# Moving the operands of an expert layer's matmuls within SBUF: four pools, each with a pad of its own

## The chip, the cores and the metric

The kernel runs on one core of a Trainium2 chip. The metric is device time in microseconds of one execution. Three executions of the kernel before gave 1094.63, 1095.49 and 1096.83 us; the median, 1095.49 us, is what the change is compared with. TensorE is called PE below, with PEld for its loads of stationary operands; VectorE is DVE, ScalarE ACT, GpSimd POOL and SyncE SP.

## The reference

Causal attention with two sparse masks (half of the heads see the last 32 positions, the other half every 32nd), and behind it a mixture of 8 experts in which each token goes to its best two:

```python
scores = np.where(masks[None], scale * np.matmul(q, k.transpose(0, 1, 3, 2)), -1e9)
attn = softmax(scores)                       # q, k, v: (8, 8, 576, 64)
x = np.matmul(attn, v)  ->  (4608, 512)      # one row per token
top2, top2_w = best two of  x @ w_gate + log1p(exp(x @ w_noise)) * noise
for e in range(8):
    for k in range(2):
        mask = top2[:, k] == e
        h = np.maximum(x[mask] @ w1[e], 0.0)              # 512 -> 1024
        out[mask] += top2_w[mask, k, None] * (h @ w2[e])  # 1024 -> 512
```

All inputs and the output are float32.

## The kernel before

**Two parts on one instruction stream.** The attention of 8 batches, with the routing of each batch behind it, and the experts are cut into pieces (class `Piece`), and `issue_all` (L291 to L406) puts them out in an order worked out from planned durations and dependences. Where a tile lies in memory is no input to that order. Attention ends near 330 us; from there on the experts' matmuls alone fill PE. Some jobs of the first three experts run earlier, between the attention's pieces.

**A job** is a part of one expert's list of tokens, 256 to 384 rows wide. The rows are gathered by indirect DMA on POOL's queue into `xg` (L971), turned by DVE into `xr` (L1010), and split into two float32r halves: `xhi` is the value rounded by ACT's cast (L1017), `xlo` the rest, by DVE (L1019). Weights come from HBM on SP's queue into `wraw` and are split in the same way into `w1hi`, `w1lo`, `w2hi`, `w2lo` (L894, L895).

**Layer 1** (L1048): for each of the 8 slices f of 128 hidden columns, 12 matmuls into one PSUM bank: for each d of 4, (w1hi, xhi), (w1hi, xlo), (w1lo, xhi). The 128x128 piece of the weights is the stationary operand, the 256 to 384 tokens are the moving one. Where the job has a tail, the program reads the list's length and runs the ten inner matmuls of the 12 at one of three widths. ACT then writes `hhi` (relu, L1067), DVE `hlo` (L1072).

**Layer 2** (L1110): for each block of 128 tokens, 24 matmuls into one bank: for each f of 8, (hhi, w2hi), (hhi, w2lo), (hlo, w2hi). Here 128 columns of h are stationary and 512 columns of w2 move. DVE weighs the result (L1135), POOL's queue scatters it (L1140).

So the x tiles and the w2 tiles are moving operands, the w1 tiles and the h tiles are stationary.

**Where the tiles lie.** SBUF pools stand one behind the other in the order in which they are opened, tiles within a pool in the order of their first use, and each tile takes a multiple of 32 bytes per partition. In the program before, the pools that matter are `wring` (`wraw`, `w1hi`, `w1lo`, `w2hi`, `w2lo`; all tiles 2048 bytes per partition) and behind it `ffn` (the lists, `xg`, `xhi`, `xlo`, `hhi`, `hlo`, `prev`, `xr`). The places of the matmul operands, as bytes behind a multiple of 128:

| operand | role | first byte before | behind a multiple of 128 |
|---|---|---|---|
| w1hi, w1lo | stationary, layer 1 | 111,264 | 32 |
| xhi, xlo | moving, layer 1 | 181,184 | 64 |
| hhi, hlo | stationary, layer 2 | 193,472 | 64 |
| w2hi, w2lo | moving, layer 2 | 144,032 | 32 |

All these tiles are a multiple of 128 bytes long, and so is every step by which a matmul's slice starts within one (a slice of 128 columns is 512 bytes, a slice d of x 1536), so each row of the table holds for every matmul.

Of the kernel before, what the change touches and what calls it, by code (L numbers as in the profile page):

```python
# [9 lines left out]
F32 = mybir.dt.float32  # L10
F32R = mybir.dt.float32r
# [11 lines left out]
def kernel(  # L23
# [31 lines left out]
    NF = FF // 128  # L55
# [92 lines left out]
    actx = ctx.enter_context(ExitStack())  # L148
    keep = actx.enter_context(tc.tile_pool(name="keep", bufs=1))
    wring = actx.enter_context(tc.tile_pool(name="wring", bufs=4))  # L150
    ffn = actx.enter_context(tc.tile_pool(name="ffn", bufs=1))
    psum = actx.enter_context(tc.tile_pool(name="psum", bufs=1, space=PSUM))

    kT_l = keep.tile([128, STRIDE + S], F32, name="kT_l")
# [70 lines left out]
    def ring(pool, shape, dtype, name, k):  # L225
        return Ring(k, make=lambda: pool.tile(shape, dtype, name=name, bufs=k))
# [189 lines left out]
    R = {}  # L416
# [452 lines left out]
    for name, shape, dtype, depth in (  # L869
            ("tabt", [128, 3, 3], I32, 3), ("gix", [128, 3], I32, 3), ("tabx", [128, 12, 3], I32, 2),  # L870
            ("gxx", [128, 3, 4], I32, 2), ("xg", [128, 4, 128], F32, 2), ("xr", [128, ND * 128], F32, 1),
            ("xhi", [128, ND, WID], F32R, 1), ("xlo", [128, ND, WID], F32R, 1),
            ("hhi", [128, WID], F32R, NF), ("hlo", [128, WID], F32R, NF),
            ("prev", [128, DM], F32, 4)):
        R[name] = ring(ffn, shape, dtype, name, depth)
    for layer in (1, 2):
        for part in ("hi", "lo"):
            R[f"w{layer}{part}"] = ring(wring, [128, 512], F32R, f"w{layer}{part}", NF)
    R["wraw"] = ring(wring, [128, 512], F32, "wraw", 5)
    ER = 1000000  # L880
    ZC = 384
# [407 lines left out]
```

## Time and profile before

| | before |
|---|---|
| time, median of 3 (lowest to highest) | 1095.49 us (1094.63 to 1096.83) |
| span of the profiled execution | 1098.7 us |
| PE busy | 1062.6 us, 97% of the span |
| matmuls on PE | 8637, of which the experts' (L1048 and L1110) are 3072 and 1792 |
| DVE, POOL, ACT busy | 607.4, 566.9 and 435.3 us |

The profiled execution is one of its own, 3.2 us above the median. A busy PE is not PE at its peak: a matmul counts from its start until its result has left the array, so one begins while the one before still counts as busy. How fast PE goes is read from the distance between starts. The chain of work that ended last lists which instruction, or which wait, set the end, in order of time. A line of a timeline gives start and duration in us, then engine, line, operation, tiles written and read, and sizes (K by M of the stationary operand, then the result).

### The profile page before, as it was taken

The numbers are of one execution on the slowest core, as the hardware profiler recorded it, in microseconds if no ns is written. First come the engines' busy times: TensorE is split into PE (matmuls) and PEld (weight loads), VectorE is DVE, ScalarE is ACT, GpSimd is POOL, SyncE is SP. The second block draws the span as 40 slices with busy tenths as digits, with TensorE's granted clock in tenths as the row PEclk, the third lists the DMA queues.
The fourth block names the chain that finished last, engine by engine and source line by source line (L and its number), as shares of the span: only waits on it lengthen the run. The fifth ranks groups of instructions, "written<-read, shape, count | busy, mean of one in ns | idle before, by whom it ended". The sixth has DMA issues, their size and how long they took to land.

```text
span 1098.7 us, 23347 instructions
## 1 busy us (share of the span) xinstructions
PE 1062.6 (97%) x8637; PEld 938.2 (85%) x8637; DVE 607.4 (55%) x1604; ACT 435.3 (40%) x1135; POOL 566.9 (52%) x741
## 2 busy tenths in 40 slices
PE   8898998999999999999999999999999999999995
PEld 7677787788889888989998989898988898898994
DVE  6688988686573236536673455345534653373341
ACT  5689988775552114214341233123312331141120
POOL 1044543552535556647676556554656464657520
PEclk8998899999999999999999999999999999999998
DMA  7899999998653324424553236224522452253210
GB/s 167 216 214 222 245 220 222 207 240 236 171 166 104 100 75 142 153 72 146 176 177 108 75 107 184 73 71 121 171 79 66 126 164 75 76 153 97 78 50 23
DMA packets 169710, 152.95 MB, mean 139 GB/s; under 512 B 52879, under 2 KB 137359, under 8 KB 169576
## 3 DMA queue, kind: packets, MB, share of 16 engines
q1 hardware_dynamic: 145160, 92.31, 33.5%
q0 software_dynamic: 24416, 58.87, 17.5%
q8 instruction: 82, 1.34, 0.5%
q14 instruction: 52, 0.43, 0.1%
HBM read 112.78 MB, written 39.39 MB: 138 GB/s over the span
## 4 chain that ended last, share of the span: by engine, by line
PE 87%; ACT 5%; DMA 4%; DVE 2%; issue 1%; POOL 0%; SPq 0%; POOLq 0%; DVEq 0%; ACTq 0%
PE bankB L1110 6%; PE bankG L1110 6%; PE bankE L1110 5%; PE bankE L1048 5%; PE bankC L1048 5%; PE bankF L1048 5%; PE bankD L1048 5%; PE bankA L1048 5%; PE bankB L1048 5%; PE bankC L1110 5%; PE bankH L1048 5%; PE bankD L1110 5%; PE bankG L1048 5%; PE bankF L1110 4%; PE bankH L1110 4%; PE bankA L1110 4%
## 5 line engine op out<-in xcount | busy, mean ns | idle before, releaser
L971 POOL DMA_INDIRECT xg<-x_dram,gxx x248 | 254.7, 1027 | 110.0 <-issue 56.5
L1140 POOL DMA_INDIRECT out_dram<-prev,tabt x80 | 82.4, 1030 | 100.9 <-DVE prev L1135 46.8
L824 POOL DMA_INDIRECT tab<-ent,addr x96 | 94.0, 979 | 64.0 <-issue 18.5
L1088 POOL DMA_INDIRECT prev<-out_dram,gix x80 | 78.6, 982 | 91.5 <-issue 36.2
L1010 DVE STREAM_TRANSPOSE xr<-xg 128x512 f32<-128x512 f32 (+1 forms) x66 | 68.6, 1040 | 11.3 <-DMA xg<-x_dram,gxx 10.0
L1017 ACT CAST xhi<-xr 128x512 fp32r<-128x512 f32 (+1 forms) x66 | 39.0, 592 | 72.3 <-DVE xr L1010 72.3
L894 ACT CAST w2hi<-wraw 128x512 fp32r<-128x512 f32 x80 | 47.1, 619 | 25.4 <-PE bankA L1119 7.4
L895 DVE TENSOR_TENSOR w1lo<-wraw,w1hi 128x512 fp32r<-128x512 f32 x80 | 54.8, 687 | 2.8 <-ACT w1hi L894 0.2
L895 DVE TENSOR_TENSOR w2lo<-wraw,w2hi 128x512 fp32r<-128x512 f32 x80 | 52.7, 684 | 5.1 <-ACT w2hi L894 4.7
L1019 DVE TENSOR_TENSOR xlo<-xr,xhi 128x512 fp32r<-128x512 f32 (+1 forms) x66 | 43.5, 659 | 19.2 <-ACT xhi L1017 17.9
L894 ACT CAST w1hi<-wraw 128x512 fp32r<-128x512 f32 x80 | 49.0, 615 | 0.1
L812 POOL COPY ent<-wt 96x12 f32<-96x12 f32 x8 | 1.6, 196 | 89.2 <-DVE wt L806 89.2
L1048 PE MATMUL bankE<-xhi,w1hi 128*128 128x256 f32 (+3 forms) x132 | 39.8, 301 | 0.0
L1067 ACT ACTIVATE hhi<-bankC 128x256 fp32r<-128x256 f32 (+2 forms) x32 | 13.7, 428 | 65.0 <-PE bankC L1048 65.0
L1048 PE MATMUL bankE<-xhi,w1lo 128*128 128x256 f32 (+3 forms) x132 | 39.4, 299 | 0.0
L1048 PE MATMUL bankE<-xlo,w1hi 128*128 128x256 f32 (+3 forms) x132 | 39.3, 298 | 0.0
L1067 ACT ACTIVATE hhi<-bankA 128x256 fp32r<-128x256 f32 (+2 forms) x32 | 13.6, 424 | 63.6 <-PE bankA L1048 62.6
L1048 PE MATMUL bankC<-xhi,w1hi 128*128 128x256 f32 (+3 forms) x128 | 38.6, 302 | 0.0
L1048 PE MATMUL bankH<-xhi,w1hi 128*128 128x256 f32 (+3 forms) x128 | 38.6, 301 | 0.0
L1067 ACT ACTIVATE hhi<-bankH 128x256 fp32r<-128x256 f32 (+2 forms) x32 | 13.5, 423 | 62.7 <-PE bankH L1048 62.7
L1048 PE MATMUL bankF<-xhi,w1hi 128*128 128x256 f32 (+3 forms) x128 | 38.4, 300 | 0.0
L1048 PE MATMUL bankD<-xhi,w1hi 128*128 128x256 f32 (+3 forms) x128 | 38.4, 300 | 0.0
(660 smaller groups left out, 3640.5 us busy)
## 6 DMA issues: line engine op xcount, KB each, us to landing
wraw<-in_moe_w_dram SPq DMA_DIRECT2D x160, 256.0 KB
out_dram<-zeros SPq DMA_DIRECT2D x12, 768.0 KB
ks<-in_k_dram SPq DMA_DIRECT2D x15, 320.0 KB
qs<-in_q_dram SPq DMA_DIRECT2D x15, 320.0 KB
vraw<-in_v_dram SPq DMA_DIRECT2D x30, 160.0 KB
raw<-in_k_dram SPq DMA_DIRECT2D x16, 288.0 KB
v_l<-in_v_dram SPq DMA_DIRECT2D x16, 288.0 KB
raw<-in_q_dram SPq DMA_DIRECT2D x16, 288.0 KB
```

The lines of the kernel that those rows point to most:

```text
L824: st = nc.gpsimd.indirect_dma_start(out=tab, out_offset=bass.IndirectOffsetOnAxis(ap=s["addr"].t[:, t, kk:kk + 1], axis=0), in_=s["ent"].t ...
L894: Piece("ACT", act(512) + 30, lambda o: nc.scalar.copy(hi.t, raw.t), rank, read=[raw], alloc=[hi], expert=True)
L895: Piece("DVE", dve(512), lambda o: nc.vector.tensor_tensor(lo.t, raw.t, hi.t.bitcast(F32), ALU.subtract), rank, read=[raw, hi], alloc=[lo] ...
L971: dma(lambda o, g=g: nc.gpsimd.indirect_dma_start(out=xg.t[:, g, :], out_offset=None, in_=x_dram[:4 * known, :], in_offset=bass.IndirectOf ...
L1010: Piece("DVE", 8 * rows, lambda o, xg=xg, xr=xr, ng=ng, rows=rows: nc.vector.transpose(xr.t.rearrange("p (c x) -> p c x", c=ND)[:, :, :row ...
L1017: Piece("ACT", act(4 * rows), lambda o, view=view, cols=cols: nc.scalar.copy(xh.t[:, :, cols], view()), rank, read=[xr], expert=True, **{h ...
L1019: Piece("DVE", dve(4 * rows), lambda o, view=view, cols=cols: nc.vector.tensor_tensor(xl.t[:, :, cols], view(), xh.t[:, :, cols].bitcast(F ...
L1048: nc.tensor.matmul(ps.t[:, :width], a.t[:, 128 * d:128 * d + 128], c.t[:, d, :width], start=(m == 0), stop=(m == len(todo) - 1))
L1067: Piece("ACT", act(width) + 30, lambda o: nc.scalar.activation(hh.t[:, :width], ps.t[:, :width], AF.Relu), rank, read=[ps], alloc=[hh], ex ...
L1088: dma(lambda o: nc.gpsimd.indirect_dma_start(out=pv.t[:rows, :], out_offset=None, in_=out[:known, :], in_offset=bass.IndirectOffsetOnAxis( ...
L1110: nc.tensor.matmul(ps.t, HT[n, f][p[0]].t[:, cols], W2[n][f][p[1]].t, start=(m == 0), stop=(m == len(todo) - 1))
L1140: st = nc.gpsimd.indirect_dma_start(out=out[:known, :], out_offset=bass.IndirectOffsetOnAxis(ap=tb.t[:rows, i, 0:1], axis=0), in_=pv.t[:ro ...
```

## The change

The pool `wring` is split: `w2hi` and `w2lo` go to a pool of their own, `w2ring`. The pool `ffn` is split: `hhi` and `hlo` go to `hpool`. Each of the four pools gets, as its first tile, a pad of one partition that nothing writes or reads: 32 bytes in `wring`, 64 in `w2ring`, 96 in `ffn`, 128 in `hpool`. No instruction is added, taken away or moved, and no tile changes its size or number of buffers.

```diff
     wring = actx.enter_context(tc.tile_pool(name="wring", bufs=4))
+    w2ring = actx.enter_context(tc.tile_pool(name="w2ring", bufs=1))
     ffn = actx.enter_context(tc.tile_pool(name="ffn", bufs=1))
+    hpool = actx.enter_context(tc.tile_pool(name="hpool", bufs=1))
+    for pool, name, words in ((wring, "shift_w1", 8), (w2ring, "shift_w2", 16), (ffn, "shift_x", 24),
+                              (hpool, "shift_h", 32)):
+        pool.tile([1, words], F32, name=name, bufs=1)
     psum = actx.enter_context(tc.tile_pool(name="psum", bufs=1, space=PSUM))
...
-        R[name] = ring(ffn, shape, dtype, name, depth)
-    for layer in (1, 2):
+        R[name] = ring(hpool if name in ("hhi", "hlo") else ffn, shape, dtype, name, depth)
+    for layer, pool in ((1, wring), (2, w2ring)):
         for part in ("hi", "lo"):
-            R[f"w{layer}{part}"] = ring(wring, [128, 512], F32R, f"w{layer}{part}", NF)
+            R[f"w{layer}{part}"] = ring(pool, [128, 512], F32R, f"w{layer}{part}", NF)
```

## The prediction

> **What bounds the kernel now.** First the page: the busy shares and the chain of work that ended last.
>
> ```profile
> span 1098.7 us, 23347 instructions
> PE 1062.6 (97%) x8637; PEld 938.2 (85%) x8637; DVE 607.4 (55%) x1604; ACT 435.3 (40%) x1135; POOL 566.9 (52%) x741
> PE 87%; ACT 5%; DMA 4%; DVE 2%; issue 1%; POOL 0%; SPq 0%; POOLq 0%; DVEq 0%; ACTq 0%
> ```
>
> PE makes 87% of the chain, but an average hides stages. So next the table by stretches, whole, then for layer 1 (L1048) and for layer 2 (L1110) alone, cut at 330 us, where attention ends:
>
> ```profile
> core 0: us, PE busy (x) PEld busy (x) DVE busy (x) ACT busy (x) POOL busy (x), PEclk, DMA share, GB/s
> 0.00:330.00 330.00, 306.90 (x4212) 257.25 (x4213) 249.70 (x976) 237.69 (x719) 130.95 (x257) 0.95 0.87 210
> 330.00:1098.00 768.00, 755.70 (x4427) 680.99 (x4425) 357.70 (x629) 197.57 (x417) 435.90 (x484) 1.00 0.36 109
> ...
> 0.00:330.00 330.00, 45.02 (x291) 40.43 (x292) 0.95 0.87 210
> 330.00:1098.00 768.00, 379.29 (x2783) 376.70 (x2781) 1.00 0.36 109
> ...
> 0.00:330.00 330.00, 44.72 (x168) 29.90 (x168) 0.95 0.87 210
> 330.00:1098.00 768.00, 383.94 (x1624) 303.76 (x1624) 1.00 0.36 109
> ```
>
> Behind 330 us PE is busy 755.7 of 768 us at full granted clock (1.00); the 12.3 us that lack are the end, behind the last matmul. No other engine is over 57% busy there, and the experts' matmuls fill the stretch (379.3 + 383.9 us). Ahead of 330 us, DMA is at 0.87 of its engines and only 459 of these matmuls run. So the question is whether one of the experts' matmuls becomes shorter or longer. Nothing else of the change can count for much.
>
> Busy time doesn't say how fast PE goes; the distance between starts does. From the timeline, the first matmul of a bank and the first of the next (12 matmuls later), for widths 384, 320 and 256, and 12 matmuls of layer 2 with width 512:
>
> ```profile
> 329.58 0.34 PE L1048 MATMUL bankC<-xhi,w1hi 128*128 128x384 f32 x1
> 331.66 0.34 PE L1048 MATMUL bankB<-xhi,w1hi 128*128 128x384 f32 x1
> ...
> 409.80 0.31 PE L1048 MATMUL bankG<-xhi,w1hi 128*128 128x320 f32 x1
> 411.55 0.31 PE L1048 MATMUL bankE<-xhi,w1hi 128*128 128x320 f32 x1
> ...
> 699.83 0.40 PE L1110 MATMUL bankD<-w2hi,hlo 128*128 128x512 f32 x1
> 702.63 0.40 PE L1110 MATMUL bankD<-w2hi,hlo 128*128 128x512 f32 x1
> 702.87 0.28 PE L1048 MATMUL bankC<-xhi,w1hi 128*128 128x256 f32 x1
> 704.27 0.28 PE L1048 MATMUL bankB<-xhi,w1hi 128*128 128x256 f32 x1
> ```
>
> The chain shows the same as whole groups (start, length, engine, bank, line, matmuls):
>
> ```profile
> 340.14 2.08 PE bankA L1048 x12
> ...
> 411.72 1.76 PE bankE L1048 x12
> ...
> 461.20 5.60 PE bankD L1110 x24
> ```
>
> One matmul takes 2.08/12 = 173.3 ns at 384 columns, 1.76/12 = 146.7 at 320, 1.40/12 = 116.7 at 256, and 5.60/24 = 233.3 at 512. From 320 to 384 columns a column costs 26.7/64 = 0.417 ns, so 384 columns should take 160.0. **13.3 ns of each of these matmuls don't depend on the width.** By the same 0.417 ns a column, 13.3 ns are 32 columns, and 32 columns of 4 bytes are a run of 128 bytes in each partition. At 256 columns the excess is 116.7 - 106.7 = 10.0 ns (three quarters of such a run), at 512 it is 233.3 - 213.3 = 20.0 ns (one and a half). Over all matmuls of the two lines, counted by width (1856 of 256, 288 of 320, 768 of 384, 160 of 288, which is near enough to 320 to go with it; 1792 of 512), that is 18.6 + 16.2 + 35.8 = 70.6 us.
>
> **Where the excess sits.** The last matmul ahead of a gap in the loads shows whether a stationary operand that is being loaded holds up the matmul that streams beside it:
>
> ```profile
> 238.21 0.34 PE L1048 MATMUL bankC<-xhi,w1hi 128*128 128x384 f32 x1
> 238.21 0.19 PEld L1048 LDWEIGHTS bankC<-xlo,w1hi 128*128 128x128 f32 x1
> ...
> 238.56 0.34 PE L1048 MATMUL bankC<-xhi,w1lo 128*128 128x384 f32 x1
> ...
> 238.83 0.20 PEld L617 LDWEIGHTS bankA<-v_s,aT 72*64 72x64 f32 x4 [0.26 <-ACT w2hi L894]
> ```
>
> The matmul at 238.21 has a load beside it, the one at 238.56 has none for 0.27 us. Both last 0.34 us; without 13.3 ns the second would show 0.33. So the excess belongs to the moving stream, not to a meeting with the next load. The table of places says what differs between the layers: x starts 64 bytes behind a multiple of 128, w2 starts 32 behind. A moving operand of n whole runs of 128 bytes that starts off such a multiple touches n + 1 of them. That is just the one run of excess in layer 1, and it is the reading on which I forecast.
>
> **The change part by part.** No instruction comes, goes or moves; each pad has no reader and no writer. What moves is the place of tiles. `wring` began at 101,024, 32 bytes behind a multiple of 128; with its pad of 32, `wraw`, `w1hi` and `w1lo` stand at 64. Their 21 tiles of 2048 bytes end at 144,064, and 64 bytes later w2 stands at 144,128, at 0. It ends at 176,896; with 96 of pad, 192 for `tabt` and 96 for `gix`, `xg` stands at 177,280, and x at 181,376, at 0. `hpool` begins at 204,352, and h at 204,480, at 64. So the change does what its words say; that it doesn't I leave out of the chances.
>
> The price of a matmul after it: the least that can stay above the columns' time I take from a place where attention's transposes run one behind the other, 128 columns each:
>
> ```profile
> 23.40 0.60 PE L688 MATMUL bankG<-ident,xo 128*128 128x128 f32 x4
> ...
> L688 PE MATMUL bankG<-ident,xo x4: 270/272/275, 23.4 to 23.7; 128*128 128x128 f32 x4
> ```
>
> (a line of the timeline, then the same four with their least, median and greatest ns). The fourth starts 600 - 272 = 328 ns behind the first, so they follow at 109 ns; 256 steps of 0.417 are 106.7 ns (such a float32 column takes two steps), and some 2.5 ns stay. So one run of 13.3 ns goes at 288 to 384 columns down to 2.5 (10.8 saved), at 256 the whole 10.0 down to 2.5 (7.5 saved), at 512 one run of the one and a half (13.3 saved, 6.7 stay: I don't know what the half is). The bounds of each saving are what it would be at 2.5 ns left everywhere (17.5 at 512), and below nothing as in the rivals. The sum: 1856 x 7.5 = 13.9 us, 1216 x 10.8 = 13.1 us, 1792 x 13.3 = 23.9 us, together 50.9.
>
> Of this, 459 of 4864 matmuls, about 4.8 us, lie ahead of 330 us among attention's waits, where DMA's 0.87 may take back what PE saves; I count half. That leaves 48.5 us, and 1098.7 - 48.5 = 1050.2 us of span. The median of the runs lies 3.2 us below this profiled span: **1047 us**.
>
> What is late next? PE's own waits are short and all in attention, the longest sum being
>
> ```profile
> PE bankG L688 <- DVE xo L641: 3.5, 2, 3.2
> ```
>
> so nothing is near to holding PE behind 330 us: the rewriting of x and w1 for the next job lies beside three blocks of layer 2 (16.8 us, then about 15.8), and takes DVE at most 8 casts of weights,
>
> ```profile
> L895 DVE TENSOR_TENSOR w1lo<-wraw,w1hi 128x512 fp32r<-128x512 f32 x80 | 54.8, 687 | 2.8 <-ACT w1hi L894 0.2
> ```
>
> 5.5 us. The other tiles that move (`wraw`, `xg`, `xr`, `prev`) are read and written by DMA, ACT and DVE, which have 57% of load or less behind 330 us; I cost them at nothing. Ahead of it that cover is thin: were all DMA there 1% slower or faster, that would be about 3 us either way.
>
> The Trainium skill speaks against this change. "TensorE: Matmul & The Clock Gate", Part 2, says that PE has two independent read ports, so that loading the next stationary operand takes nothing from the running matmul. The two rows at 238 us agree, 0.34 us with and without a load, and by that rule the stationary side of the change is worth nothing. "SBUF — State Buffer", Specifications, gives 16 bytes as the unit in which SBUF is read; 0, 32 and 64 are all multiples of 16, so by that page nothing changes at all, which is the second rival below. The first page's section on the back-to-back gap gives N/2.4 + 2.5 ns, 215.8 at 512 columns, where the rows here have 233.3; an estimate with it for all widths would give 58 us of saving, and 1040 us.
>
> **The rivals.**
> - **No change, 1095.5 us.** The excess is a fixed cost of such a matmul. For it: 256 and 512 columns cost the same per column (0.456 ns), though x and w2 lie at different places, and the excess there is no whole number of runs. Against: exactly one run at 320 and 384.
> - **Only places off a multiple of 64 cost.** Then x at 64 was well placed before, and only w2 (at 32) gains: half a run, 1792 x 6.7 = 12.0 us, or a whole one, 23.9; less half of the early tenth, 1084 or 1073 us. For it: layer 2 has the greater excess.
> - **Slower, 1115 us.** The extra half run of layer 2 comes with its stationary operand at 64, where layer 1 has it at 32. The change puts w1 at 64 as well, so all 3072 matmuls of layer 1 would pay 6.7 ns more: 20.5 us, less half of the early tenth 19.5. This decides if the moving operand's place turns out to be worth nothing and the stationary one's is not. For it: 20.0 against 13.3 ns, which the moving place alone doesn't explain. Against: the matmul at 238.56.
>
> **How the numbers follow.** Forecast 0.40, no change 0.28, only off 64 0.13, slower 0.19. The forecast's own range is 1036 (all down to 2.5 ns, early ones too: 58.4 us saved, and 1 us for the scatter of runs) to 1060 (the 256-column matmuls keep their excess: 13.9 us less saved). The range over 8 in 10 runs from there to the top of no change, 1098; the slower case stays outside. A measurement of this kernel tells 0.2%, about 2 us, from no change. Faster 0.53, same 0.28, slower 0.19.
>
> **What would show it.** In the profile after, a group of 24 in layer 2 takes about 5.28 us instead of 5.60, one of 12 at 384 columns 1.95 instead of 2.08, at 256 about 1.31 instead of 1.40. Unchanged groups mean the first of the rivals; 5.28 to 5.44 with 2.08 kept means the second; 2.16 at 384 columns the third. The forecast is wrong in its second step if the groups shrink and the span doesn't: then a wait on PE must have appeared behind 330 us.

## The result, and the profile after

| | before | after |
|---|---|---|
| time, median of 13 runs | 1096.83 us | 1092.37 us |
| ratio after / before | | 0.9947, 95% interval 0.9924 to 0.9969 |
| span of the profiled execution | 1098.7 us | 1095.7 us |

The change makes the kernel faster by 0.5%: by the ratio, which compares runs that stand beside each other, 5.8 us of 1096.83 (3.4 to 8.3 by its interval); the two medians alone differ by 4.5. The forecast was 48.5 us, to 1047. The 13 runs before include the three given further up. The ratios here and below leave out one execution of 2057 us after, another of 2057 us of `both_best`, and one of 1433 us of the kernel before beside it, and no trace shows what held these up.

The page after, and then the same three views by stretches as before: whole, layer 1 (now L1053), layer 2 (now L1115).

```profile
span 1095.7 us, 23347 instructions
PE 1060.5 (97%) x8637; PEld 943.4 (86%) x8637; DVE 607.3 (55%) x1604; ACT 435.9 (40%) x1135; POOL 562.6 (51%) x741
...
330.00:1095.00 765.00, 752.65 (x4438) 684.41 (x4436) 358.47 (x632) 198.15 (x418) 435.12 (x488) 1.00 0.36 110
...
330.00:1095.00 765.00, 381.04 (x2784) 378.64 (x2784) 1.00 0.36 110
...
330.00:1095.00 765.00, 379.38 (x1634) 305.29 (x1632) 1.00 0.36 110
```

PE still fills everything behind 330 us (752.7 of 765 us, the rest being the end), and nothing new waits there. So nothing was gained and then lost: the matmuls themselves hardly became shorter. The chain shows by how much (start, length, engine, bank, line, matmuls):

```profile
425.97 5.51 PE bankG L1115 x24
431.47 5.49 PE bankE L1115 x24
440.63 2.10 PE bankH L1053 x12
```

24 matmuls of layer 2 take 5.49 to 5.51 us, where it was 5.60; the forecast had 5.28. Twelve of layer 1 at 384 columns take 2.10, where it was 2.08; the forecast had 1.95. The mean distance between the starts of neighbouring matmuls, over all such pairs of the two traces that follow without a pause, says it more finely:

| columns (layer) | matmuls | before, ns | after, ns | forecast, ns | difference over all, us |
|---|---|---|---|---|---|
| 256 (1) | 1856 | 116.7 | 117.0 | 109.2 | +0.4 |
| 288, 320 (1) | 448 | 133.3, 146.7 | 132.8, 146.1 | 122.5, 135.8 | -0.3 |
| 384 (1) | 768 | 173.5 | 174.7 | 162.5 | +0.9 |
| 512 (2) | 1792 | 233.2 | 229.2 | 220.0 | -7.2 |

The sum is -6.2 us, which the interval of the measured ratio holds. The whole gain is 4.0 ns in each matmul of layer 2. The two profiled spans differ by 3.0 us only: the last matmul of attention and routing ends at 323.5 us before and at 326.0 after, and from there to the experts' last matmul it is 762.2 and 756.7 us.

### The profile page after: what moved, and what is told of

Same layout as the page of the kernel before. It is cut to its first block, busy times and chain, and to the rows that moved or that the text cites. A ratio compares the mean times of both kernels' runs of the same rounds, so it can differ in the third digit from the quotient of the medians.

```text
span 1095.7 us, 23347 instructions
## 1 busy us (share of the span) xinstructions
PE 1060.5 (97%) x8637; PEld 943.4 (86%) x8637; DVE 607.3 (55%) x1604; ACT 435.9 (40%) x1135; POOL 562.6 (51%) x741
## 4 chain that ended last, share of the span: by engine, by line
PE 88%; ACT 4%; DMA 4%; DVE 3%; issue 1%; SPq 0%; POOL 0%; POOLq 0%; ACTq 0%; DVEq 0%
PE bankB L1115 6%; PE bankG L1115 6%; PE bankE L1053 5%; PE bankE L1115 5%; PE bankC L1053 5%; PE bankH L1053 5%; PE bankF L1053 5%; PE bankA L1053 5%; PE bankD L1053 5%; PE bankB L1053 5%; PE bankC L1115 5%; PE bankG L1053 5%; PE bankD L1115 5%; PE bankF L1115 4%; PE bankH L1115 4%; PE bankA L1115 4%
## 5 line engine op out<-in xcount | busy, mean ns | idle before, releaser
L976 POOL DMA_INDIRECT xg<-x_dram,gxx x248 | 251.8, 1015 | 111.1 <-issue 58.4
L1024 DVE TENSOR_TENSOR xlo<-xr,xhi 128x512 fp32r<-128x512 f32 (+1 forms) x66 | 43.5, 659 | 19.2 <-ACT xhi L1022 17.8
L1053 PE MATMUL bankE<-xhi,w1hi 128*128 128x256 f32 (+3 forms) x132 | 39.9, 302 | 0.0
L1053 PE MATMUL bankE<-xhi,w1lo 128*128 128x256 f32 (+3 forms) x132 | 39.6, 300 | 0.0
L1053 PE MATMUL bankE<-xlo,w1hi 128*128 128x256 f32 (+3 forms) x132 | 39.4, 299 | 0.0
L1053 PE MATMUL bankC<-xhi,w1hi 128*128 128x256 f32 (+3 forms) x128 | 38.7, 303 | 0.0
L1053 PE MATMUL bankH<-xhi,w1hi 128*128 128x256 f32 (+3 forms) x128 | 38.7, 302 | 0.0
L1053 PE MATMUL bankF<-xhi,w1hi 128*128 128x256 f32 (+3 forms) x128 | 38.5, 301 | 0.0
L1053 PE MATMUL bankD<-xhi,w1hi 128*128 128x256 f32 (+3 forms) x128 | 38.5, 301 | 0.0
L1053 PE MATMUL bankB<-xhi,w1hi 128*128 128x256 f32 (+3 forms) x128 | 38.5, 300 | 0.0
```

The lines of the kernel that those rows point to most:

```text
L976: dma(lambda o, g=g: nc.gpsimd.indirect_dma_start(out=xg.t[:, g, :], out_offset=None, in_=x_dram[:4 * known, :], in_offset=bass.IndirectOf ...
L1024: Piece("DVE", dve(4 * rows), lambda o, view=view, cols=cols: nc.vector.tensor_tensor(xl.t[:, :, cols], view(), xh.t[:, :, cols].bitcast(F ...
L1053: nc.tensor.matmul(ps.t[:, :width], a.t[:, 128 * d:128 * d + 128], c.t[:, d, :width], start=(m == 0), stop=(m == len(todo) - 1))
```

## The experiments

The medians of the kernel before, measured beside these runs, lay between 1101 and 1152 us. The traces of the experiments show where such differences sit for the most part: the last matmul of attention and routing ends anywhere between 320 and 365 us. So kernels run once are compared by the same two measures as above, the groups of the chain and the mean distance of starts in the experts' matmuls. All kernels come from the changed one. Places are given as bytes behind a multiple of 128 or 256. Below, the stream is the reading of the moving operand, column after column, and its walk is the way that this takes through memory; the load is the reading of the stationary operand; the columns' time is 0.417 ns for each column, as in the prediction, and the floor is the 2.5 ns that it found above that time between transposes.

### Is it the place within 128 bytes? Four layouts

The pads alone differ. With the pools split, but w1 32, x 64, h 64, w2 32 as before (`split_only`):

```diff
-    for pool, name, words in ((wring, "shift_w1", 8), (w2ring, "shift_w2", 16), (ffn, "shift_x", 24),
-                              (hpool, "shift_h", 32)):
+    for pool, name, words in ((hpool, "shift_h", 16),):
```

> The pools are split as in the change, but padded so that every operand keeps its place of before behind a multiple of 128 bytes (w1 32, x 64, h 64, w2 32); only the distance between the tiles in whole runs of 128 bytes changes. Theory A (the place within 128 bytes sets the excess over the columns' time): layer 2 goes back to 233.3 ns a matmul (20.0 ns of excess), layer 1 stays at 173.3 at 384 columns, and the time is that of before. Theory B (the coarse distance between the pools did it): layer 2 stays near the 229.2 ns of the changed kernel.

with pads of 96, 0, 96 and 64 bytes, all four operands at 0 (`all_at_0`):

> All four operands start at a multiple of 128 bytes. Theory A1 (the moving operand's place alone counts): layer 2 keeps the 229.2 ns of the changed kernel and layer 1 its 174.7 at 384 columns, since the moving places are the same. Theory A2 (what counts is how far the stationary operand lies from the moving one within 128 bytes, because the load and the stream meet in memory): both layers change, with the distance 64 gone to 0, by several ns a matmul, and in the same direction in both layers. Theory A3 (the stationary place alone counts): both layers change, too.

with 96, 64, 96 and 0, stationary at 0 and moving at 64 (`st0_mv64`):

> The changed kernel's places exchanged: stationary operands at 0, moving ones at 64 bytes behind a multiple of 128. Theory A2 (distance): the distance is 64 again, so layer 2 stays at 229.2 ns and layer 1 at 174.7 ns at 384 columns. Theory A1 (moving place): layer 1 goes back to 173.3 ns, as with x at 64 before; layer 2 moves away from 229.2. Theory A3 (stationary place): both layers as in the kernel with all at 0.

and with 32, 0, 64 and 64, layer 1 at the places that layer 2 had, and the other way round (`places_swapped`):

> Layer 1 gets the places that layer 2 had before (stationary 64, moving 32), layer 2 those of layer 1 (stationary 32, moving 64). Theory A1: layer 2 loses the half run that w2 at 32 cost, 226.7 ns (13.3 of excess), layer 1 gains it, 180 ns at 384 columns. Theory A2 with the sign of the distance counting: the same. If the excess of a layer is its own, whatever the places (the theory of no change): 233 and 173 ns.

| kernel | layer 1 (stationary, moving) | 256, ns | 384, ns | layer 2 (stationary, moving) | 512, ns |
|---|---|---|---|---|---|
| before | 32, 64 | 116.7 | 173.5 | 64, 32 | 233.2 |
| split_only | 32, 64 | 116.7 | 173.5 | 64, 32 | 233.2 |
| after | 64, 0 | 117.0 | 174.7 | 64, 0 | 229.2 |
| all_at_0 | 0, 0 | 118.9 | 175.7 | 0, 0 | 232.5 |
| st0_mv64 | 0, 64 | 114.5 | 174.3 | 0, 64 | 233.2 |
| places_swapped | 64, 32 | 119.8 | 176.6 | 32, 64 | 234.1 |

`split_only` gives the numbers of before in every column. So splitting the pools does nothing by itself; what counts is where the pads put the tiles. Places do count, but over all of these layouts layer 2 moves by 4.9 ns and layer 1 at 384 columns by 3.1 ns. None of them comes near to the floor, 215.8 and 162.5. The moving operand's place alone explains nothing: in layer 2 the same moving place, 0, gives 229.2 and 232.5, in layer 1 it gives 174.7 and 175.7. Nor does the stationary one's alone (64 in layer 2 gives 233.2 and 229.2), nor the distance of the two within 128 bytes: `st0_mv64` has the 64 of after in layer 2, and 233.2 ns. With all operands at 0 not even one run of 128 bytes went away.

### Whose is the excess? One column instead of a walk

```diff
-nc.tensor.matmul(ps.t[:, :width], a.t[:, 128 * d:128 * d + 128], c.t[:, d, :width], start=(m == 0),
+nc.tensor.matmul(ps.t[:, :width], a.t[:, 128 * d:128 * d + 1].to_broadcast([128, 128]), c.t[:, d, :width], start=(m == 0),
...
-nc.tensor.matmul(ps.t, HT[n, f][p[0]].t[:, cols], W2[n][f][p[1]].t, start=(m == 0),
+nc.tensor.matmul(ps.t, HT[n, f][p[0]].t[:, cols], W2[n][f][p[1]].t[:, :1].to_broadcast([128, 512]), start=(m == 0),
```

> Based on the changed kernel. Layer 1's stationary operand is one column read 128 times, so its load touches one place in memory instead of 512 bytes; layer 2's moving operand is one column read 512 times. The products are therefore other ones than the reference's. Theory M (the excess comes from the load of the next stationary operand and the moving stream meeting in memory): layer 1 loses most of its excess, to about 163 ns at 384 columns and 109 at 256, and layer 2 as well, to about 216 ns. Theory S (the moving stream alone is slowed by walking through memory): layer 1 stays at 174.7 and 117, layer 2 falls to about 216. Theory F (a fixed cost of a float32r matmul, nothing to do with memory): both stay, 174.7 and 229.

`one_moving_column` has it the other way round (`c.t[:, d, :1].to_broadcast([128, width])` and `HT[n, f][p[0]].t[:, cols.start:cols.start + 1].to_broadcast([128, 128])`).

> The other way round: layer 1's moving operand is one column read 256 to 384 times, layer 2's stationary operand one column read 128 times; the products are other ones than the reference's. Theory M: both layers lose most of the excess (about 163 ns at 384 columns, 216 in layer 2). Theory S: layer 1 loses it, layer 2 keeps its 229 ns. Theory F: both stay.

The chain of `one_stationary_column` (layer 1's load reads one place, layer 2's stream reads one place):

```profile
470.76 2.08 PE bankH L1053 x12
...
432.50 5.18 PE bankB L1115 x24
```

and that of `one_moving_column` (layer 1's stream reads one place, layer 2's load does):

```profile
465.11 1.95 PE bankH L1053 x12
...
426.15 5.56 PE bankB L1115 x24
```

Where the stream stays in one place, the excess is gone but for the floor: 215.8 ns at 512 columns, 162.5 at 384, 2.5 ns over the columns' time each. Where the load stays in one place, the excess is still there: 173.4 ns at 384 and 231.5 in layer 2. From 320 columns up this is theory S: but for the floor, the prediction's 13.3 and 20.0 ns are a cost of the moving stream as it walks through memory. At 256 columns it is less clear. With the stream in one place 111.6 ns are left, 4.9 above the columns' time, and with the load in one place 114.4, where it was 117.0 after. So there the load has a share of some 2.6 ns.

The third kernel of that set kept layer 2's operands in bfloat16:

```diff
-            ("hhi", [128, WID], F32R, NF), ("hlo", [128, WID], F32R, NF),
+            ("hhi", [128, WID], BF16, NF), ("hlo", [128, WID], BF16, NF),
...
-            R[f"w{layer}{part}"] = ring(pool, [128, 512], F32R, f"w{layer}{part}", NF)
+            R[f"w{layer}{part}"] = ring(pool, [128, 512], F32R if layer == 1 else BF16, f"w{layer}{part}", NF)
...
```

(two instructions that read these tiles as float32 are adapted as well).

> Layer 2's operands are kept in bfloat16 (its result is less exact), at the changed kernel's places, with half the bytes to load and to stream per matmul; layer 1 is untouched. Theories M and S: with half the bytes the excess of layer 2 shrinks to the 2 to 3 ns seen between transposes, 216 ns a matmul. Theory F, if the fixed cost belongs to any matmul of this size: it stays near 227 to 229 ns; if it belongs to float32r alone, 216 too.

```profile
445.12 5.18 PE bankF L1115 x24
```

The median distance in layer 2 was 216 ns, layer 1 stayed at 174.8 at 384 columns. In bfloat16, with 2 bytes a column, the walk costs nothing. This run alone can't tell the number of bytes from the type, and the load is halved in it, too; that float32r as such has no fixed cost is shown by the kernels with one column.

### Or does it take a load to meet? A quarter of the load

```diff
+M = 32 if 0 < m < len(todo) - 1 else 128
-nc.tensor.matmul(ps.t[:, :width], a.t[:, 128 * d:128 * d + 128], c.t[:, d, :width], start=(m == 0),
+nc.tensor.matmul(ps.t[:M, :width], a.t[:, 128 * d:128 * d + M], c.t[:, d, :width], start=(m == 0),
```

and the same in layer 2.

> The changed kernel, but all matmuls except the first and the last of a sum have a stationary operand of 32 columns instead of 128, so that a quarter of the load runs beside the same moving stream; three quarters of the output's sums lack those products. If the excess is a meeting of load and stream, it falls to about a quarter: some 165 ns at 384 columns and 218 in layer 2. If it belongs to the moving stream alone, 173 to 175 and 229 to 233 ns stay.

From its timeline, layer 2 with loads of 32 columns, and a group of its chain:

```profile
499.94 0.39 PE L1117 MATMUL bankC<-w2hi,hhi 128*32 128x512 f32 x1
499.94 0.11 PEld L1117 LDWEIGHTS bankC<-w2lo,hhi 128*32 128x32 f32 x1
500.17 0.40 PE L1117 MATMUL bankC<-w2lo,hhi 128*32 128x512 f32 x1
...
430.16 5.57 PE bankB L1117 x24
```

The load is down from 0.19 to 0.11 us, the next matmul still starts 0.23 us later: 231.7 ns on average, and 174.6 at 384 columns. There the size of the load is not the matter. At 256 columns it is in part: 114.1 ns, 2.9 less than after, much as with the load in one place.

### How long is a run? Short walks

```diff
-nc.tensor.matmul(ps.t, HT[n, f][p[0]].t[:, cols], W2[n][f][p[1]].t, start=(m == 0),
+nc.tensor.matmul(ps.t.rearrange("p (r x) -> p r x", x=32), HT[n, f][p[0]].t[:, cols],
+                 W2[n][f][p[1]].t[:, None, :32].to_broadcast([128, 16, 32]), start=(m == 0),
```

The same few columns are read over and over: in `short_walk` 32 in layer 2 and, in the same way, 4 in layer 1; in the other two 16 in layer 1 and 8 in layer 2, and 32 and 64.

> Based on the changed kernel. Layer 1's moving operand is the same 4 columns (16 bytes) over and over, layer 2's the same 32 columns (128 bytes); the products are other ones than the reference's. Theory S1 (each new column that is read from memory costs, however near to the last): both layers keep their excess, 174.7 ns at 384 columns and about 230 ns in layer 2. Theory S2 (the stream pays where it crosses into another run of memory, of 64 or 128 bytes): layer 1 falls to about 162.5 ns, as with one column; layer 2, if the run is 128 bytes or more, falls to about 216, and keeps part of the excess if it is 64.

> Layer 1's moving operand is the same 16 columns (64 bytes) over and over, layer 2's the same 8 columns (32 bytes); the products are other ones than the reference's. With 16 bytes there was no excess, with 128 bytes 23.2 ns at 512 columns. If the stream pays on leaving a run of 64 bytes, both show none (162.5 and 216 ns) as long as each stays within one; if on leaving 32, layer 1 shows some 17 ns at 384 columns and layer 2 none.

> Layer 1's moving operand is the same 32 columns (128 bytes), layer 2's the same 64 columns (256 bytes); the products are other ones than the reference's. From 23.2 ns at 512 columns with 128 bytes, layer 1 should have 17 ns at 384 (177 ns). Layer 2 with 256 bytes: as with the whole walk, 229 to 233 ns, if the cost is one for each run entered; clearly less than with 128 bytes (under 20 ns) if jumping back is what made 23.2.

One group each of `short_walk` (4 columns in layer 1), of `walk_64_32` (16 columns in layer 1, 8 in layer 2), and of `walk_128_256` (64 columns in layer 2):

```profile
440.38 1.95 PE bankH L1053 x12
```

```profile
473.14 2.13 PE bankD L1053 x12
...
457.18 5.18 PE bankG L1116 x24
```

```profile
466.20 5.51 PE bankG L1116 x24
```

| columns walked | bytes | layer, columns | ns | above the columns' time, ns |
|---|---|---|---|---|
| 1 | 4 | 2, 512 | 215.8 | 2.5 |
| 4 | 16 | 1, 384 | 162.5 | 2.5 |
| 8 | 32 | 2, 512 | 216.3 | 2.9 |
| 16 | 64 | 1, 384 | 178.0 | 18.0 |
| 32 | 128 | 1, 384 | 177.8 | 17.8 |
| 384 | 1536 | 1, 384 | 174.7 | 14.7 |
| 32 | 128 | 2, 512 | 236.6 | 23.2 |
| 64 | 256 | 2, 512 | 229.1 | 15.7 |
| 512 | 2048 | 2, 512 | 229.2 | 15.9 |

Up to 32 bytes the walk is free; from 64 bytes on all of the excess is there, and with 64 and 128 bytes some 3 to 7 ns more than in the whole walk. So what the stream reads again for nothing is at least 32 bytes and less than 64. A run of 32 bytes, or 8 columns of 4 bytes, is the simplest reading; two shorter runs that are both kept would look the same. The 32 bytes were tried in layer 2 alone, the 64 in layer 1 alone. At 512 columns there are 64 runs of 32 bytes: (229.2 - 215.8) / 64 = 0.21 ns each after, and (233.2 - 215.8) / 64 = 0.27 before. At 384 columns, 48 runs, it was (173.5 - 162.5) / 48 = 0.23. These are means and no fixed price: after, at 256 columns it is (117.0 - 111.6) / 32 = 0.17, at 288 (132.8 - 122.5) / 36 = 0.29. And layer 2 in bfloat16 walks through 32 such runs in each matmul and pays nothing. So it may be the rate, 4 bytes a column, that is too high, and not the step into a run that costs; no run here separates the two.

### Where the 4 ns of layer 2 come from

Five layouts whose pads move the operands by 128 bytes and more. `best_of_seen` (pads 96, 0, 32 and 64) has layer 2 at the changed kernel's places within 128 bytes and layer 1 at stationary 0, moving 64:

> Layer 1 at the places where its 256-column matmuls were shortest so far (stationary 0, moving 64), layer 2 at those where it was shortest (stationary 64, moving 0: the changed kernel's). If each layer's times depend on its own two places alone: 114.5 ns at 256 columns, 174.3 at 384, 229.2 in layer 2, and from 380 us on some 11 us less than the kernel before. If the layers disturb each other through the rest of the layout, other numbers.

`h_back_128` drops h's pad of 128:

> The changed kernel with the pad of 128 bytes in front of h taken out: h starts 128 bytes earlier, still 64 behind a multiple of 128; nothing else moves. If places within 128 bytes are what counts: layer 2 stays at 229.2 ns. If a run of 256 bytes or more counts (the theory after the last four runs, where the same places within 128 gave 233.3): layer 2 goes to 233.3 ns and the change's gain in it is gone. Layer 1 stays at 174.7 and 117.0 either way.

`h_on_256` makes it 384:

> The changed kernel with h moved on by 256 bytes, nothing else moved. If the pattern repeats after 256 bytes: layer 2 stays at 229.2 ns. If it is longer (512 or more): another number, most likely 232 to 234. Layer 1 stays.

`both_on_128` has pads of 32, 192, 224 and 0:

> The changed kernel with w2 128 bytes further on and h moved so that the distance of the two stays the same within 256 bytes (h 64, w2 128 behind a multiple of 256); layer 1's operands keep their places within 256 bytes. If the distance counts, layer 2 stays at 229.2 ns; if the place of one of them counts, it goes to 232 to 234 ns.

`both_best` has 96, 0, 160 and 64:

> Layer 1 at the places within 256 bytes at which its 256-column matmuls took 114.5 ns (w1 0, x 192), layer 2 at those of the changed kernel (h 192, w2 0). If places within 256 bytes are what counts: 114.5, 174.3 and 229.2 ns together, some 11 us less on PE from 380 us on than before, a ratio of about 0.990 to the kernel before; the changed kernel has 0.9947. If not, layer 1 or layer 2 shows other numbers and the ratio lies nearer to 1.

The chain of `h_back_128`, then that of `h_on_256`, then that of `both_on_128`:

```profile
426.94 5.59 PE bankG L1114 x24
432.53 5.60 PE bankE L1114 x24
```

```profile
431.93 5.51 PE bankG L1114 x24
437.44 5.49 PE bankE L1114 x24
```

```profile
433.81 5.50 PE bankB L1114 x24
439.31 5.49 PE bankF L1114 x24
```

128 bytes on one operand, which leave every place within 128 bytes as it was, take the gain away; 256 bytes leave it. In layer 2, by the distance of h from w2 within 256 bytes:

| distance | kernels (h, w2 within 256) | ns |
|---|---|---|
| 32 | before, split_only (192, 160) | 233.2 |
| 64 | h_back_128, best_of_seen (64, 0); st0_mv64 (128, 64) | 233.2 to 233.3 |
| 96 | places_swapped (32, 192) | 234.1 |
| 128 | all_at_0 (128, 0) | 232.5 |
| 192 | after, h_on_256, both_best (192, 0); both_on_128 (64, 128) | 229.2 to 229.8 |

Four layouts with a distance of 192 have the gain and seven with another have none of it, `both_on_128` with both places changed and the distance kept among the four. So the load's place does reach the stream, by some 2% at most, through the distance of the two within 256 bytes. The whole gain needs the whole load: at the same distance of 192 layer 2 takes 231.7 ns with a quarter of the load and 231.5 with the load in one place. Why the distance acts so stays open.

Layer 1 doesn't follow its distance as well. At 256 columns it took 117.0 ns after, 115.2 in `h_back_128`, where neither w1 nor x moved, and 114.5, 115.5 and 116.1 in `st0_mv64`, `both_best` and `both_on_128`, all at a distance of 64. In `best_of_seen` it was not the 114.5 that was expected but 117.7; there the distance in layer 1 is 192 within 256 bytes, and layer 2, expected at 229.2, has 233.3 at its distance of 64. What goes before it seems to set which rhythm it falls into; that wasn't tried by itself and stays open.

`both_best`, run 12 times, has a ratio of 0.994 to the kernel before (0.9913 to 0.9967): the expected 0.990 lies outside, and it is no better than the change (0.9947).

## Why the prediction was wrong, point by point

- **What bounds the kernel**: right. PE's matmuls behind 330 us set the time before and after, and no wait took the place of what was saved.
- **The size of the excess**: right. 70.6 us lie above the columns' time. With the stream in one place the matmuls show the floor that the transposes gave (215.8 and 162.5 ns), but at 256 columns 4.9 ns stay. So the walk makes some 54 us of it, where the prediction's floor of 2.5 ns everywhere leaves 58.
- **Whose it is**: right from 320 columns up. The reading of the matmul at 238.56, that lasts as long with no load beside it, holds: its record is 338 ns long, and with the stream in one place the median at this width is 326. `one_stationary_column` and `narrow_load` keep nearly all of the excess there, and lose 2.6 to 2.9 of 10.3 ns at 256 columns.
- **What it is**: wrong, and here the forecast failed. The step was: "A moving operand of n whole runs of 128 bytes that starts off such a multiple touches n + 1 of them. That is just the one run of excess in layer 1, and it is the reading on which I forecast." With x at a multiple of 128, a matmul of 384 columns is 14.7 ns above its columns' time (174.7 - 160), where it was 13.5 above it. What the runs show in its place is a cost along the stream's way, 0.2 to 0.3 ns on average for each 32 bytes that it walks through. A stream of the same length walks through as many of them from any start that is a multiple of 32, and all tiles of this kernel start at such. That the excess is about 13.3 ns, the time of 32 columns or 128 bytes, at 320 and at 384 columns is then chance, and why it doesn't grow between these two stays open. The 10.0 ns at 256 and 20.0 at 512, which grow with the width, spoke for a cost along the way, and the prediction has them under its first rival.
- **The sum**: of 13.9, 13.1 and 23.9 us the runs left nothing of the first two (+0.4 and +0.6) and 7.2 of the third. Those 7.2 come from another place: the distance of h and w2 within 256 bytes. The forecast had no such term, so that the kernel got faster at all is luck: the four pads happened to make that distance 192.
- **The rivals**: no change was right in its mechanism, "a fixed cost of such a matmul", as far as place is concerned, and 0.5% off in the result. (The prediction's paragraph on the Trainium skill calls it the second rival; it stands first in the list.) "Only places off a multiple of 64" named the layer that gained, but its groups were to be 5.44 us or less, and h_back_128 keeps w2 at 0 and has no gain. The slower rival, 6.7 ns for a stationary operand at 64, isn't there: with w1 at 64 and x at 0 layer 1 changed by -0.6 to +1.2 ns.
- **The moved DMA tiles and the early tenth**: too small to be seen. The last matmul of attention and routing ends 2.5 us later after than before, but in the nine other layouts of the same instructions it ends anywhere between 320.5 and 359.4 us.

The Trainium skill's "TensorE: Matmul & The Clock Gate", Part 2, has two read ports of PE that don't take from each other. `narrow_load` agrees for the bulk (a quarter of the load, the same stream), and the 4.0 ns by the distance of the two operands are what it doesn't tell. "SBUF — State Buffer", Specifications, of the same Trainium skill gives SBUF lines of 16 bytes and a penalty for each step into a new one. That the walk costs agrees; but 32 bytes, two such lines, are read over and over for nothing (216.3 ns at 512 columns) and only 64 are dear (178.0 at 384), and the measurement decides.

## What to carry to other kernels

An excess that equals some round quantity at two widths is no evidence for that quantity: fit it over all widths first, and here 256 and 512 said that it grows with the stream. Whether an operand's walk costs anything is found with one kernel that reads a single column instead; that should come before any work on where tiles lie. Placing tiles is worth a try only where matmuls of float32r fill the time, is worth 0.5% here, and the distance between the two operands within 256 bytes has to be tried, not the place of each within 128.

## What the runs showed of the hardware that wasn't expected

- A float32r moving stream that walks through memory pays, on average, 0.17 to 0.29 ns for each 32 bytes: at 512 columns 229 to 234 ns, against 215.8 from one column, 216.3 from 32 bytes over and over, and 216 in bfloat16.
- The distance between stationary and moving operand, within 256 bytes, changes a matmul of 512 columns by up to 4.9 ns (229.2 to 234.1), and moving both operands by 128 bytes, or one by 256, changes nothing. A load a quarter of the size makes it longer by 2.5 ns (231.7 against 229.2).
- At 256 columns a smaller load makes a matmul shorter by 2.6 to 2.9 ns (114.4 and 114.1 against 117.0), at 384 by 0.1 to 1.3 ns (174.6 and 173.4 against 174.7).
- Starts follow a rhythm: before, those of layer 2 were alternately 232 and 235 ns apart; after, they went 226, 229 and 232 ns in turn.
